# A decode step's output projection: seven rows to a partition in two wo tiles, and their other rows in 8 KB pieces by indirect loads

## The chip, the cores and the metric

The kernel runs on one core of a Trainium2 chip. The metric is the device time of one launch in microseconds. Five engines work side by side: PE (TensorE, matrix products), DVE (VectorE), ACT (ScalarE), POOL (GpSimd) and SP (SyncE, which here only issues transfers). Sixteen DMA engines move data between the chip's memory and the core's on-chip memory of 128 partitions.

## The reference

One decode step of a transformer block with adaptive layer norm, batch 8, width 512, all in float32. The matrix that this change is about is `wo`, of 4096 rows by 512 columns.

```python
W = min(4096, max(256, Sk // 4))          # 2048 of the 8192 cached positions
mod = (silu(c) @ w_mod).reshape(8, 6, 1, 512)
sa, ca, ga, sb, cb, gb = (mod[:, i] for i in range(6))
h = layernorm(x) * (1 + ca) + sa
q = (h @ wq)                              # 32 heads of 128; 8 KV heads
k, v = last W positions of k_cache, v_cache, each KV head for 4 heads
p = softmax(q @ k.T * 128 ** -0.5)
o = (p @ v)                               # (8, 1, 4096)
x = x + ga * (o @ wo)
h = layernorm(x) * (1 + cb) + sb
x = x + gb * (relu(h @ w1 + b1) ** 2 @ w2 + b2)
```

## The kernel before

**Transfers.** Nearly all of the bytes are the caches: K and V of eight KV heads, each in two tiles of 4 MB (`("K", n)` and `("V", n)`, n from 0 to 15). They go into four big slots of one buffer, `home`. A fifth, small slot of 2 MB (`small`) takes in turn the second part of `w_mod`, the wo tiles 0, 1 and 2, the tile `far`, and a part of `w1`. The fourth wo tile comes with the last weights, in a big slot (`tail`). The list `loads` gives the order; `pump` issues the next load of the list as soon as a slot of its size is free, and `done(key)` gives a slot back and pumps. The issues are written into SP's queue in this order, and each waits there for the last reader of its slot.

**Work.** The main loop runs over 37 half-tile steps `s`. In step s, DVE transposes K tile s // 2 (`transposes`, L216), PE makes scores (`scores`, L387) and, five steps later (`PV_LAG`), the weighted sums over V (`weighted`, L473); the soft-max of one KV head is spread over the steps after its scores (`soft_a` to `soft_g`). Every fourth step `gather` turns one head group's result into `oT`, which has, for 128 partitions and 8 chunks i, a column for each batch: partition p, chunk i stands for row 8p + i or, in the first tile, another order (below). Every eighth step `project_o(j)` (L526) multiplies `oT` with wo tile j, of 1024 rows, and adds into `wo_ps`. It runs at steps 14, 22 and 30 for j = 0, 1, 2, and after the loop for j = 3.

**The first wo tile before.** Its 1024 rows are 32 blocks of 32 rows. Of each block, 28 rows go to four partitions, seven rows each (14 KB to a partition, one load); the other four rows of every block, 128 rows in all, make the tile `far`, of 8 KB pieces. The pieces are loaded by three DMAs on SP's queue: two of 12 partitions (L143) and one of 8 (L144), in the partitions 0 to 11, 32 to 43, and 3, 7, ... 31. GpSimd clears half of the slot first (L139). In `project_o(0)`, seven matmuls take the seven chunks, and four matmuls with the selection matrix `fsel` (L537) put the eighth chunk's values into the places of the pieces (`oX`, by two ACT copies). `far_rows` (L549), at step 18, multiplies them with the far tile: eight matmuls, four over 64 partitions and four over 32. `gather` writes the columns in the matching order when `hk < 2`, that is for the first wo tile.

**The second wo tile before** has eight rows to a partition (16 KB), one load (L133), and eight matmuls.

**The end.** After the loop come the last projection, the second layer norm, the MLP with w1 and w2 (L690 takes the 14 chunks of w2, whose last pieces are the last loads of all), and the store of y (L700). The biases b1 and b2 are loaded on ACT's queue by two DMAs, four partitions each (L563).

Of the kernel before, what the change touches and what calls it, by code (L numbers as in the profile page):

```python
# [8 lines left out]
F32 = mybir.dt.float32  # L9
AF = mybir.ActivationFunctionType  # L10
ALU = mybir.AluOpType
# [2 lines left out]
EPS = 1e-5  # L14
BIG_SLOTS = 4
PV_LAG = 5


@with_exitstack
def tile_adaln_cached_attention_mlp(  # L20
# [14 lines left out]
    nc = tc.nc  # L35
    P = 128
    B, HKV, SK, DH = k_cache.shape
    D = wq.shape[0]
    HQ = wq.shape[1] // DH
    REP = HQ // HKV  # L40
# [8 lines left out]
    H = P // 2  # L49
# [3 lines left out]
    consts = ctx.enter_context(tc.tile_pool(name="consts", bufs=1))  # L53
    work = ctx.enter_context(tc.tile_pool(name="work", bufs=2))
    ktp = ctx.enter_context(tc.tile_pool(name="ktp", bufs=2))
    ps_m = ctx.enter_context(tc.tile_pool(name="ps_m", bufs=2, space=bass.MemoryType.PSUM))
# [8 lines left out]
    for q in range(D // P):  # L65
        b = slice(32 * q, 32 * q + B)
        nc.scalar.dma_start(xc_in[b], xc[b])

    ident = consts.tile([P, P], F32, name="ident")
    make_identity(nc, ident)  # L70
    ones = consts.tile([P, P], F32, name="ones")
    nc.gpsimd.memset(ones, 1.0)
    eps = consts.tile([P, 1], F32, name="eps")
    nc.vector.memset(eps, EPS)
    fsel = consts.tile([P, 4, P], F32, name="fsel")
    nc.gpsimd.memset(fsel, 0.0)
    for y in range(2):
        nc.gpsimd.tensor_copy(
            fsel[:, :, 32 * y : 32 * y + 12].rearrange("p r (q a) -> p r q a", a=4),
            ident.rearrange("p (y a r q) -> p y r q a", y=2, a=4, r=4)[:, y, :, :3],  # L80
        )
    nc.gpsimd.tensor_copy(
        fsel[:, :, H : H + 32].rearrange("p r (h x) -> p r h x", x=4)[..., 3],
        ident.rearrange("p (h r q) -> p r h q", r=4, q=4)[..., 3],
    )
    oX = consts.tile([P, 8, 32], F32, name="oX")

# [2 lines left out]
    base = [3 * big, 0, big, 2 * big]  # L92
# [10 lines left out]
    def load(key):  # L103
        kind, i = key
        held[key] = free[size_of(key)].pop(0)
        if key == ("wq", 0):
            return
        t = slots[size_of(key)][held[key]]
        if kind in "KV":

            hk, c = divmod(i, 2)
            v = k_cache[4 * c : 4 * c + 4, hk] if kind == "K" else v_cache[c::2, hk]
            v = v[:, SK - W :, :].rearrange("u (p j) d -> p u (j d)", j=NJ)
            cuts = (0, big // 2, big) if key == ("V", 2 * HKV - 1) else (0, big)
            for x, y in zip(cuts, cuts[1:]):
                nc.sync.dma_start(t[:, x:y], v[..., x:y])
            return

        def rows(o, v):
            n = v.shape[1] * v.shape[2]  # L120
            nc.sync.dma_start(t[:, o : o + n].rearrange("p (a n) -> p a n", n=v.shape[2]), v)

        w1v = w1.rearrange("(p kc) n -> p kc n", p=P)

        def wo_rows(j):

            r = 2 * REP * DH
            if j == 0:
                v = wo[:r].rearrange("(b s) n -> b s n", s=32)[:, :28].rearrange("b (g i) n -> b g (i n)", i=7)
                nc.sync.dma_start(t[:, : 7 * D], v)  # L130
                return
            v = wo[j * r : (j + 1) * r, :].rearrange("(p i) n -> p (i n)", p=P)
            nc.sync.dma_start(t[:, : big // 2], v)  # L133

        if kind == "wo":
            wo_rows(i)
        elif kind == "far":

            nc.gpsimd.memset(t[:H], 0.0)  # L139
            v = wo[: 2 * REP * DH].rearrange("(h q s) n -> q h s n", q=4, s=32)[:, :, 28:]  # L140
            v = v.rearrange("q h r n -> q h (r n)")
            for y in range(2):
                nc.sync.dma_start(t[32 * y : 32 * y + 12, : 4 * D], v[:3, 4 * y : 4 * y + 4])  # L143
            nc.sync.dma_start(t[3:32:4, 4 * D :], v[3])  # L144
        elif kind == "mod":

            v = w_mod.rearrange("(p kc) n -> p (kc n)", p=P)
            nc.sync.dma_start(t, v[:, big:] if i else v[:, :big])
        elif kind == "wq":

            o = base[held["wq", 0]]
            nc.sync.dma_start(home[:, o : o + 2 * big], wq.rearrange("(p k) n -> p (k n)", p=P))
        elif kind == "tail":
            wo_rows(HKV // 2 - 1)
            rows(big // 2, w1v[:, 0:2])
        elif kind == "w1":
            rows(0, w1v[:, 2:4])
        else:
            v = w2.rearrange("(p c) n -> p c n", p=P)
            for lo, hi in ((0, 8), (8, 12), (12, 13), (13, 14)):  # L160
                rows(D * lo, v[:, lo:hi])

    def slot(key, n, o=0):

        t = slots[size_of(key)][held[key]][:, o:]
        return t[:, : t.shape[1] // n * n].rearrange("p (a n) -> p a n", n=n)

    loads = [("mod", 0), ("mod", 1), ("wq", 0), ("wq", 1), ("K", 0), ("K", 1)]
    for n in range(2, 2 * HKV):
        if n == 9:  # L170
            loads.append(("far", 0))
        if n in (4, 11, 13):
            loads.append(("wo", (4, 11, 13).index(n)))
        loads += [("K", n), ("V", n - 2)]
    loads += [("V", 2 * HKV - 2), ("V", 2 * HKV - 1), ("tail", 0), ("w1", 0), ("w2", 0)]
    at = [0]
# [6 lines left out]
    def done(*keys):  # L183
        for k in keys:
            free[size_of(k)].append(held.pop(k))
        pump()
# [81 lines left out]
    for k in (2, 3, 4):  # L268
        n = 1 << k
# [223 lines left out]
    def gather(hk):  # L493

        o = OS_.pop(hk)
        b = slice(H * (hk % 2), H * (hk % 2) + H)
        pp = ps_m.tile([P, 512], F32, name="m_ps", tag="m_ps")
        for x in range(2):
            to = pp[b].rearrange("p (d x e i) -> p x e d i", x=2, e=2, i=8)[:, x]
            cuts = [(to, o.rearrange("p e (d i) -> p e d i", i=8))]  # L500
            if hk < 2:
                o = o.rearrange("p e (q s) -> p (e q) s", s=32)
                cuts = [
                    (to[..., :7], o[:, :, :28].rearrange("p a (g i) -> p a g i", i=7)),
                    (to[..., 7].rearrange("p e (r q) -> p e q r", r=4), o[:, :, 28:]),
                ]
            for dest, src in cuts:
                nc.tensor.matmul(dest, pick[:, x].rearrange("p t u -> p (t u)"), src, start=True, stop=True)  # L508
        tr = work.tile([P, 2, 8, 32], F32, name="tr", tag="b", bufs=1)
        nc.vector.transpose(  # L510
            tr[b].rearrange("p e i (x d) -> p (e i) x d", x=2),
            pp[b].rearrange("p (d x e i) -> p (e i) x d", x=2, e=2, i=8),
        )
        nc.vector.tensor_mul(
            oT[b, :, :B].rearrange("p i (w e) -> p e i w", e=2),
            tr[b, :, :, :4],
            RZ_[hk][b].rearrange("p (w e) -> p e w", e=2)[:, :, None, :].to_broadcast([H, 2, 8, 4]),
        )

    def project_o(j):  # L520

        last = j == HKV // 2 - 1
        key = ("tail", 0) if last else ("wo", j)
        w = slot(key, D)
        for i in range(8 if j else 7):
            nc.tensor.matmul(  # L526
                wo_ps[32 * (i % 4) : 32 * (i % 4) + 32, :],
                oT[:, i, :],
                w[:, i, :],
                start=(j == 0 and i < 4),  # L530
                stop=(last and i >= 4),
            )
        if j == 0:

            px = ps_m.tile([P, 512], F32, name="m_ps", tag="m_ps")
            for r in range(4):
                nc.tensor.matmul(px[:, 32 * r : 32 * r + 32], fsel[:, r], oT[:, 7, :], start=True, stop=True)  # L537
            px = px[:, :P].rearrange("p (r b) -> p r b", b=32)
            nc.scalar.copy(oX[:H, :4], px[:H])
            nc.scalar.copy(oX[:32, 4:], px[H : H + 32])  # L540
        if not last:
            done(key)

    def far_rows():

        w = slot(("far", 0), D)
        for r in range(8):
            k = H if r < 4 else 32
            nc.tensor.matmul(  # L549
                wo_ps[32 * (r % 4) : 32 * (r % 4) + 32, :], oX[:k, r], w[:k, r, :], start=False, stop=False  # L550
            )
        done(("far", 0))

    def late_tiles():

        late = work.tile([P, NJ, 8, 4], F32, name="pr4", bufs=1).rearrange("p j x w -> p (j x w)")
        rT = late[:, : FC * 32].rearrange("p (c b) -> p c b", b=32)
        b1_in, b2_in, x1, h2T = late[:NQ, 512 : 512 + FG], late[:NQ, 1024:1152], late[:, 1152:1280], late[:, 1280:1408]
        h2T = h2T.rearrange("p (c b) -> p c b", b=32)
        nc.gpsimd.memset(rT, 0.0)  # L560
        for t, v in ((b1_in, b1), (b2_in, b2)):
            v = v.rearrange("(g n) -> g n", g=NQ)
            nc.scalar.dma_start(t, v)  # L563
        return rT, b1_in, b2_in, x1, h2T

    window(0)
# [2 lines left out]
    for s in range(N + PV_LAG + 1):  # L569
# [16 lines left out]
            soft_f(g - 1)  # L586
        if v > C and v % (2 * C) == 1 and v < N:
            project_o(v // C // 2 - 1)
        if s == 18:
            far_rows()  # L590
        if 1 <= v <= N:
            weighted(v - 1, 1)
        if i == 0 and soft:
# [143 lines left out]
```

## Time and profile before

| | |
|---|---|
| Median of three runs | 393.38 us (393.16 to 393.44) |
| The profiled execution | 393.28 us, of which the profile's span covers 391.5 us |
| PE, DVE, ACT, POOL busy | 258.8, 224.0, 46.7, 5.9 us |
| Bytes moved | 165.04 MB, 422 GB/s over the span |
| DMA queue q1 (SP's) | 6814 packets, 164.70 MB, 98.3% of sixteen engines' span |
| Mean granted clock of PE | 0.886 |

A busy time of an engine is the sum of its instructions; the page's rows of 40 slices show where it lies. A line such as `L526 PE MATMUL wo_ps<-small,oT 128*32 128x512 f32 x16` reads: the instruction of line 526 on PE, writing `wo_ps` from `small` and `oT`, with its shapes and its count. "PEld" is PE's loading of the stationary operand, a name with q (SPq, ACTq) is the engine's queue issuing a transfer, and what stands in brackets is the idle time before an instruction and what ended it. In a table by stretches the columns are the stretch, its length, busy time and count of PE, PEld, DVE, ACT and POOL, the granted clock, the DMA engines' mean busy share and GB/s.

### The profile page before, as it was taken

How to read it: one execution, taken by the hardware profiler on the slowest of the kernel's cores; microseconds unless marked ns; L12 is line 12 of the kernel's file. 1: busy time of each engine (PE TensorE's matmuls, PEld its weight loads, DVE VectorE, ACT ScalarE, POOL GpSimd, SP SyncE). 2: the span in 40 equal slices, each digit the busy share in tenths (PEclk: the TensorE clock that was granted, in tenths of full speed). 3: DMA queues.
4: the chain of work that ended last, by engine and by line, in shares of the span. 5: the costliest groups of instructions: out<-in, count | busy, mean ns of one | idle time of the engine just before them, and what ended most of it. 6: DMA issues, size and time to landing. Idle time of an engine off the chain costs nothing.

```text
span 391.5 us, 4765 instructions
## 1 busy us (share of the span) xinstructions
PE 258.8 (66%) x2050; PEld 79.7 (20%) x2050; DVE 224.0 (57%) x314; ACT 46.7 (12%) x91; POOL 5.9 (2%) x13
## 2 busy tenths in 40 slices
PE   0080959868437873797379828783773737996896
PEld 0030210112112320232122202220221212222333
DVE  1370099878057835874577456490776357854322
ACT  0120111311003100310031003100200003004010
POOL 1000000000000000030000000000000000000000
PEclk9996889998859996999599968988796969997999
DMA  8999999999999999999999999999999999999994
GB/s 330 437 429 426 437 435 442 435 424 411 431 432 432 437 432 435 430 427 429 444 417 435 430 432 432 427 429 427 415 445 437 429 429 431 425 423 424 421 432 190
DMA packets 6915, 165.04 MB, mean 422 GB/s; under 512 B 806, under 2 KB 974, under 8 KB 1230
## 3 DMA queue, kind: packets, MB, share of 16 engines
q1 hardware_dynamic: 6814, 164.70, 98.3%
q8 instruction: 16, 0.26, 0.3%
q10 hardware_dynamic: 80, 0.04, 0.0%
q14 instruction: 5, 0.04, 0.0%
HBM read 164.67 MB, written 0.07 MB: 421 GB/s over the span
## 4 chain that ended last, share of the span: by engine, by line
DMA 59%; DVE 22%; PE 14%; issue 4%; SPq 0%; ACT 0%; DVEq 0%; ACTq 0%
DMA home<-in_A_k_cache_dram 37%; DVE kT L216 12%; DMA home<-in_A_wq_dram 9%; DMA home<-in_B_w_dram 7%; DMA home<-in_A_v_cache_dram 6%; PE s_ps L387 5%; DVE pT L453 4%; PE p_ps L418 3%; PE m_ps L332 2%; PE o_ps L473 2%; DVE pr L446 2%; DVE mx L401 1%; DVE qbd L350 1%; PE m_ps L403 1%; PE m_ps L423 1%
## 5 line engine op out<-in xcount | busy, mean ns | idle before, releaser
L216 DVE STREAM_TRANSPOSE kT<-home 128x1024 f32<-128x1024 f32 x128 | 151.3, 1220 | 81.8 <-DMA home<-in_A_k_cache_dram 77.7
L387 PE MATMUL s_ps<-kT,qst 128*32 128x512 f32 x512 | 129.1, 1075 | 18.9 <-DVE kT L216 18.5
L473 PE MATMUL o_ps<-home,pT 128*32 128x256 f32 x1024 | 70.2, 397 | 11.1 <-DVE pT L453 10.5
L473 PEld LDWEIGHTS o_ps<-home,pT 128*32 128x32 f32 x1024 | 33.8, 118 | 103.1 <-issue 61.3
L403 PE MATMUL m_ps<-ident,mx 128*1 128x128 f32 x16 | 4.3, 364 | 58.3 <-DVE mx L401 58.3
L387 PEld LDWEIGHTS s_ps<-kT,qst 128*32 128x32 f32 x512 | 14.4, 115 | 38.2 <-DVE kT L216 30.1
L453 DVE STREAM_TRANSPOSE pT<-pr 128x2048 f32<-128x2048 f32 x8 | 18.2, 2275 | 1.0 <-ACT pr L436 1.0
L436 ACT ACTIVATE pr<-pr,own 128x512 f32<-128x512 f32 x16 | 17.8, 1223 | 0.3
L430 ACT ACTIVATE pr<-p_ps,nm 128x512 f32<-128x512 f32 x8 | 5.5, 687 | 96.2 <-DVE nm L427 96.2
L397 ACT COPY ss<-s_ps 128x512 f32<-128x512 f32 x8 | 4.7, 586 | 98.1 <-issue 69.2
L332 PE MATMUL m_ps<-home,oX 128*32 128x512 f32 x64 | 9.2, 741 | 10.1 <-DMA home<-in_A_wq_dram 10.1
L375 ACT COPY qst<-q_ps 32x128 f32<-32x128 f32 x32 | 8.2, 256 | 62.9 <-PE q_ps L364 62.6
L350 DVE COPY qbd<-m_ps 32x128 f32<-32x128 f32 x8 | 3.0, 373 | 18.8 <-PE m_ps L347 18.6
L403 PEld LDWEIGHTS m_ps<-ident,mx 128*1 128x1 f32 x16 | 0.7, 81 | 63.5 <-DVE mx L401 63.5
L250 PE MATMUL m_ps<-xsum,sel 128*128 128x1 f32 x2 | 0.6, 362 | 18.5 <-DVE xsum L248 18.5
L418 PE MATMUL p_ps<-ss,perm 128*128 128x512 f32 x16 | 11.8, 829 | 0.0
L427 DVE TENSOR_SCALAR nm<-m_ps 128x1 f32<-128x1 f32 x8 | 1.3, 158 | 16.4 <-PE m_ps L423 16.4
L508 PE MATMUL m_ps<-o_sb,pick 128*64 128x256 f32 (+2 forms) x40 | 9.7, 377 | 0.9 <-DVE o_sb L491 0.9
L446 DVE TENSOR_SCALAR pr<-pr,own 128x512 f32<-128x512 f32 x16 | 9.2, 657 | 0.8 <-ACT pr L430 0.8
L510 DVE STREAM_TRANSPOSE tr<-m_ps 64x512 f32<-64x512 f32 x8 | 5.7, 714 | 5.4 <-PE m_ps L508 5.2
L490 DVE TENSOR_SCALAR o_sb<-o_ps,bit 128x128 f32<-128x128 f32 x16 | 5.2, 327 | 5.5 <-PE o_ps L473 5.4
L228 DVE TENSOR_SCALAR e_sb<-e_sb 128x128 f32<-128x128 f32 x1 | 0.2, 227 | 12.9 <-ACT e_sb L227 12.9
(134 smaller groups left out, 131.7 us busy)
## 6 DMA issues: line engine op xcount, KB each, us to landing
home<-in_A_k_cache_dram SPq DMA_DIRECT2D x16, 4096.0 KB, 36.6
home<-in_A_v_cache_dram SPq DMA_DIRECT2D x15, 4096.0 KB, 22.4
home<-in_w_mod_dram SPq DMA_DIRECT2D x1, 4096.0 KB
small<-in_A_wo_dram SPq DMA_DIRECT2D x2, 2048.0 KB, 25.4
home<-in_A_v_cache_dram SPq DMA_DIRECT2D x2, 2048.0 KB, 21.5
small<-in_w_mod_dram SPq DMA_DIRECT2D x1, 2048.0 KB
home<-in_A_wo_dram SPq DMA_DIRECT2D x1, 2048.0 KB
home<-in_B_w_dram SPq DMA_DIRECT2D x1, 2048.0 KB
```

What stands on the lines that cost most here:

```text
L216: nc.vector.transpose(KTS[q, j][:, rows], k[:, rows, 32 * j : 32 * j + 32])
L332: nc.tensor.matmul(pqs[r][32 * g : 32 * g + 32, :], hT[:, kc, :], w[:, 4 * r + g, :], start=(kc == 0), stop=(kc == NQ - 1),)
L350: nc.vector.tensor_copy(qbd[b, 4 * r : 4 * r + 4, j].rearrange("p g (b t) -> p t g b", t=REP), pT_[b].rearrange("p (t g b) -> p t g b", t= ...
L375: nc.scalar.copy(own[b, :, :, i, 0], pq[b, :P].rearrange("p (c m t) -> p c m t", c=2, t=REP))
L387: nc.tensor.matmul(s_ps[0][32 * g : 32 * g + 32, :], qst[hk % 2][:, P * (4 * c + u) + 32 * j :][:, :32], kT[:, u], start=(c == 0 and j == ...
L403: nc.tensor.matmul(MX_[hk][0:1, :P], mx, ident, start=True, stop=True)
L418: nc.tensor.matmul(sp, perm, SS_.pop(hk), start=True, stop=True)
L436: nc.scalar.mul(X_[hk][..., w], pr, own[:, w : w + 1])
L446: nc.vector.tensor_scalar(X_[hk][..., w], pr, own[:, w : w + 1], None, op0=ALU.mult)
L453: nc.vector.transpose(PT_[hk].rearrange("p e j r -> p j e r"), X_.pop(hk).rearrange("p j x w -> p j (x w)"))
L473: nc.tensor.matmul(O_[n][32 * g : 32 * g + 32, : 2 * DH], PT_[hk][:, e, j : j + 2].rearrange("p j r -> p (j r)"), vt[:, j : j + 2, :].rear ...
L508: nc.tensor.matmul(dest, pick[:, x].rearrange("p t u -> p (t u)"), src, start=True, stop=True)
```

## The change

- The second wo tile is laid out as the first: seven rows to a partition in one load, and its other 128 rows in a far tile of its own, `("far", 1)`, which passes through the small slot between wo tiles 1 and 2. `project_o(1)` has seven matmuls and the four selections, `far_rows(1)` runs at step 25. wo tile 2 is listed one K tile later.
- Both far tiles are loaded by an indirect DMA from GpSimd's queue. Each partition has a row index (`pieces`) into wo seen as 1024 rows of 8 KB; 32 partitions have a piece, the other 96 an index beyond wo's end, which is left out. The partitions come from `GROUPS`: 64 to 67, 92 to 95, 28 to 31, 16 to 19, 0 to 11, and 96, 124, 60 and 40. By the change's description this makes ten or eight pieces, over both tiles, on each of seven DMA engines.
- The indices are made on the chip: GpSimd writes them as a row with eleven iotas, a matmul with a single 1 turns it into a column, and two DVE steps store it as integers for tile 0 and tile 1.
- `fsel` follows GROUPS, with eleven copies instead of three. GpSimd clears all 128 partitions of the far tile's 8 KB instead of 64 partitions of 16 KB. `far_rows` is four matmuls over 128 partitions, and one ACT copy serves instead of two.
- b1 is loaded in three DMAs (partitions 0 and 1, 2, 3) and b2 in two.

```diff
+GROUPS = ((64, 4), (92, 4), (28, 4), (16, 4), (0, 4), (4, 4), (8, 4), (96, 1), (124, 1), (60, 1), (40, 1))
...
+    pieces = consts.tile([P, 2], mybir.dt.int32, name="pieces")
+
+    row = consts.tile([1, P], F32, name="row")
+    nc.gpsimd.memset(row, 4.0 * D)
+    ways, n = [], 0
+    for m, k in GROUPS:
+        h, q = divmod(n, 4)
+        ways.append((slice(m, m + k), h, slice(q, q + k)))
+        nc.gpsimd.iota(
+            row[:, m : m + k],
+            pattern=[[8, k]],
+            base=32 * h + 8 * q + 7,
+            channel_multiplier=0,
+            allow_small_or_imprecise_dtypes=True,
+        )
+        n += k
+    assert n == 32
+    pr_ = ps_m.tile([P, 512], F32, name="m_ps", tag="m_ps")
+    nc.tensor.matmul(pr_[:, 0:1], row, ones[0:1, 0:1], start=True, stop=True)
+    nc.vector.tensor_copy(pieces[:, 0:1], pr_[:, 0:1])
+    nc.vector.tensor_scalar(pieces[:, 1:2], pr_[:, 0:1], 2.0 * P, None, op0=ALU.add)
     nc.gpsimd.memset(fsel, 0.0)
...
+    for to, h, q in ways:
+        nc.gpsimd.tensor_copy(fsel[:, :, to], ident.rearrange("p (h r q) -> p r h q", h=8, r=4)[:, :, h, q])
...
-            if j == 0:
-                v = wo[:r].rearrange("(b s) n -> b s n", s=32)[:, :28].rearrange("b (g i) n -> b g (i n)", i=7)
+            if j < 2:
+                v = wo[j * r : (j + 1) * r].rearrange("(b s) n -> b s n", s=32)[:, :28].rearrange("b (g i) n -> b g (i n)", i=7)
                 nc.sync.dma_start(t[:, : 7 * D], v)
...
-            nc.gpsimd.memset(t[:H], 0.0)
-            v = wo[: 2 * REP * DH].rearrange("(h q s) n -> q h s n", q=4, s=32)[:, :, 28:]
-            v = v.rearrange("q h r n -> q h (r n)")
-            for y in range(2):
-                nc.sync.dma_start(t[32 * y : 32 * y + 12, : 4 * D], v[:3, 4 * y : 4 * y + 4])
-            nc.sync.dma_start(t[3:32:4, 4 * D :], v[3])
+            nc.gpsimd.memset(t[:, : 4 * D], 0.0)
+            nc.gpsimd.indirect_dma_start(
+                out=t[:, : 4 * D],
+                out_offset=None,
+                in_=wo.rearrange("(a r) n -> a (r n)", r=4),
+                in_offset=bass.IndirectOffsetOnAxis(ap=pieces[:, i : i + 1], axis=0),
+                bounds_check=wo.shape[0] // 4 - 1,
+                oob_is_err=False,
+            )
...
-        if n == 9:
-            loads.append(("far", 0))
-        if n in (4, 11, 13):
-            loads.append(("wo", (4, 11, 13).index(n)))
+        if n in (9, 13):
+            loads.append(("far", n // 13))
+        if n in (4, 11, 14):
+            loads.append(("wo", (4, 11, 14).index(n)))
         loads += [("K", n), ("V", n - 2)]
...
-            if hk < 2:
+            if hk < 4:
...
-        for i in range(8 if j else 7):
+        for i in range(8 if j > 1 else 7):
...
-        if j == 0:
+        if j < 2:
...
-            nc.scalar.copy(oX[:H, :4], px[:H])
-            nc.scalar.copy(oX[:32, 4:], px[H : H + 32])
+            nc.scalar.copy(oX[:, :4], px)
...
+    def far_rows(j):
+
+        w = slot(("far", j), D)
+        for r in range(4):
             nc.tensor.matmul(
-                wo_ps[32 * (r % 4) : 32 * (r % 4) + 32, :], oX[:k, r], w[:k, r, :], start=False, stop=False
+                wo_ps[32 * r : 32 * r + 32, :], oX[:, r], w[:, r, :], start=False, stop=False
             )
-        done(("far", 0))
+        done(("far", j))
...
-        for t, v in ((b1_in, b1), (b2_in, b2)):
+        for t, v, cuts in ((b1_in, b1, (0, 2, 3, 4)), (b2_in, b2, (0, 2, 4))):
             v = v.rearrange("(g n) -> g n", g=NQ)
-            nc.scalar.dma_start(t, v)
+            for x, y in zip(cuts, cuts[1:]):
+                nc.scalar.dma_start(t[x:y], v[x:y])
...
-        if s == 18:
-            far_rows()
+        if s in (18, 25):
+            far_rows(s // 25)
```

More of the change, by code (lines that the diff above doesn't have):

```diff
@@ L75, in tile_adaln_cached_attention_mlp @@
     fsel = consts.tile([P, 4, P], F32, name="fsel")
-    nc.gpsimd.memset(fsel, 0.0)
-    for y in range(2):
[L78 to L86, printed above, removed]
+    oX = consts.tile([P, 8, 32], F32, name="oX")
+    pieces = consts.tile([P, 2], mybir.dt.int32, name="pieces")
[18 more added lines that the diff above has]
+    nc.vector.tensor_scalar(pieces[:, 1:2], pr_[:, 0:1], 2.0 * P, None, op0=ALU.add)
+    nc.gpsimd.memset(fsel, 0.0)
+    for to, h, q in ways:
+        nc.gpsimd.tensor_copy(fsel[:, :, to], ident.rearrange("p (h r q) -> p r h q", h=8, r=4)[:, :, h, q])
     big = NJ * DH
@@ L137, in load @@
         elif kind == "far":
-            nc.gpsimd.memset(t[:H], 0.0)
-            v = wo[: 2 * REP * DH].rearrange("(h q s) n -> q h s n", q=4, s=32)[:, :, 28:]
-            v = v.rearrange("q h r n -> q h (r n)")
-            for y in range(2):
-                nc.sync.dma_start(t[32 * y : 32 * y + 12, : 4 * D], v[:3, 4 * y : 4 * y + 4])
-            nc.sync.dma_start(t[3:32:4, 4 * D :], v[3])
+            nc.gpsimd.memset(t[:, : 4 * D], 0.0)
[7 more added lines that the diff above has]
+            )
         elif kind == "mod":
@@ L538, in project_o @@
             px = px[:, :P].rearrange("p (r b) -> p r b", b=32)
-            nc.scalar.copy(oX[:H, :4], px[:H])
-            nc.scalar.copy(oX[:32, 4:], px[H : H + 32])
+            nc.scalar.copy(oX[:, :4], px)
         if not last:
             done(key)
[L544 to L548, printed above, removed]
+    def far_rows(j):
+        w = slot(("far", j), D)
+        for r in range(4):
             nc.tensor.matmul(
-                wo_ps[32 * (r % 4) : 32 * (r % 4) + 32, :], oX[:k, r], w[:k, r, :], start=False, stop=False
+                wo_ps[32 * r : 32 * r + 32, :], oX[:, r], w[:, r, :], start=False, stop=False
             )
-        done(("far", 0))
+        done(("far", j))
     def late_tiles():
```

## The prediction

> **What bounds the kernel now.** I read the page's engine row, its row of slices and its queue rows first, then the table by stretches.
>
> ```profile
> PE 258.8 (66%) x2050; PEld 79.7 (20%) x2050; DVE 224.0 (57%) x314; ACT 46.7 (12%) x91; POOL 5.9 (2%) x13
> DMA  8999999999999999999999999999999999999994
> q1 hardware_dynamic: 6814, 164.70, 98.3%
> q8 instruction: 16, 0.26, 0.3%
> DMA 59%; DVE 22%; PE 14%; issue 4%; SPq 0%; ACT 0%; DVEq 0%; ACTq 0%
> 40.00:380.00 340.00, 240.14 (x1842) 71.26 (x1834) 209.80 (x258) 42.24 (x82) 3.98 (x2) 0.88 1.00 430
> ```
>
> No compute engine is busy for more than two thirds, DMA holds 59% of the chain that ended last, and the DMA row is full from the second slice to the last but one. The last row is a stretch of 340 us: its DMA share is 1.00, at 430 GB/s. The transfers never run dry, so the kernel is 164.70 MB behind one full queue. A K tile of 4,096 KB is 9.8 us of that. An edit that leaves the bytes alone can gain only where the sixteen DMA engines do not finish together. One engine moves 430/16 = 26.9 GB/s: 8 KB is 0.305 us of one engine, 16 KB 0.61 us, 64 KB 2.44 us, 80 KB 3.05 us.
>
> Do they finish together? The same table in stretches of 1 us at the end (DMA share is the last column but one):
>
> ```profile
> 383.00:384.00 1.00, 1.00 (x4) 0.36 (x2) 0.68 (x3) 0.00 (x0) 0.00 (x0) 1.00 0.89 358
> 384.00:385.00 1.00, 1.00 (x25) 0.64 (x28) 0.00 (x0) 0.00 (x0) 0.00 (x0) 1.00 0.82 340
> 385.00:386.00 1.00, 1.00 (x45) 1.00 (x40) 0.00 (x0) 0.00 (x0) 0.00 (x0) 1.00 0.72 274
> 386.00:387.00 1.00, 0.64 (x24) 0.37 (x20) 0.00 (x0) 0.00 (x0) 0.00 (x0) 1.00 0.71 272
> 387.00:388.00 1.00, 1.00 (x40) 0.74 (x33) 0.00 (x0) 0.00 (x0) 0.00 (x0) 1.00 0.10 35
> ```
>
> They don't. Idle are 0.11 x 16 = 1.8 engines from 383 on, 2.9 from 384 and 4.5 from 385 to 387; the other eleven or twelve work to about 387.2 to 387.4. The shares add up to 3.24 us, so sixteen engines that ended together would end near 386.25: some 1.1 us is the most that a better spread can bring. Four or five engines have 2 to 3.5 us in hand.
>
> The end follows the last piece of w2 directly:
>
> ```profile
> 383.55 0.28 DVE L683 SCALAR_TENSOR_TENSOR pr<-relu 128x112 f32<-128x112 f32 x1
> 384.36 1.95 PE L690 MATMUL m_ps<-home,pr 128*32 128x128 f32 x64
> 386.67 1.72 PE L690 MATMUL m_ps<-home,pr 128*32 128x128 f32 x48 [0.36 <-DMA home<-in_B_w_dram]
> 387.96 0.16 PEld L690 LDWEIGHTS m_ps<-home,pr 128*32 128x32 f32 x8 [0.26 <-DMA home<-in_B_w_dram]
> ```
>
> L690 waits for w2 at 386.67 and again at 387.96, and only y and its store come after. Would compute take over if w2 came sooner? VectorE's last step is done at 383.83, so PE could go through 64 matmuls in 1.95 us and 48 in 1.72 - 0.26 us, and be done at 387.2 instead of 388.4. A gain of up to 1.1 us at the DMA therefore arrives at the end whole.
>
> **The change, part by part.** *Bytes.* Before, an engine carried 112 KB of wo's first tile (seven rows of 2 KB on 128 partitions, over sixteen engines) and 128 KB of the second (eight rows); the first tile's other 256 KB, the far rows, lay where three small loads put them. Now both tiles are 112 KB per engine, and 512 KB of far rows come in 64 pieces of 8 KB, by the change's description on seven engines: ten (80 KB) on four of them, eight (64 KB) on three. The sum is the same. Each of the nine engines without pieces loses 16 KB: 0.61 us earlier, and 0.305 us more for each far piece that it had. Each of the seven gains 80 - 16 = 64 KB or 48 KB, 2.44 or 1.83 us, less what it carried of the far rows before. No view of the profile names the engine of a packet, so which of the seven are among the four or five early ones is open; the price on either side is what I have. If the four with a real gain are the early ones, their 1.8 to 2.4 us fit into 2 to 3.5 us in hand, and the last engine is one of the nine: the end moves by -0.61 us. The bounds are -1.1 us (all together) and +2.44 us (a late engine that had no far rows gets ten pieces).
>
> The Trainium skill's page "DMA: Bandwidth & Descriptors" (Why a DMA increments its semaphore by 16 and not by 1) lets a load from SP use the largest count up to 16 that divides the slowest dimension of both sides. By it the two loads of 12 partitions ran on three engines and that of eight on eight, 72 KB on each of three engines; its section The descriptor swizzle, applied to the new partitions, puts the pieces on engines 0, 1, 2, 4, 7, 8 and 15, the first three being those. Three of the seven would then get -24 to -8 KB and only four 40 to 64 KB, an estimate of 1.5 to 2.4 us; the sum stays -0.6 us. The section speaks of plain loads to 128 partitions, and no run here shows it for an indirect one.
>
> *The packets' other queue.* The pieces come on GpSimd's queue between packets of q1. The nearest rows lie far apart. Queue q8's 16 packets of 16 KB take 0.3% of sixteen engines' span, 0.003 x 16 x 391.5/16 = 1.2 us each against 0.61 us by the byte. Queue q10's packets, from memory into a tile as the pieces are, stand in this answer for 5 to 14 us:
>
> ```profile
> q1 hardware_dynamic: 158, 3.85, 99.8%
> q10 hardware_dynamic: 64, 0.03, 1.2%
> ```
>
> Together 101.0% at an unbroken rate, 0.012 x 16 x 9/64 = 27 ns a packet. So a piece costs between nothing and, scaled from q8's excess of 0.6 us on 16 KB, 0.3 us beyond its bytes. I take nothing, since the destination and kind are q10's; ten pieces at 0.3 us would be 3 us on the seven.
>
> *The far loads and who waits.*
>
> ```profile
> 168.80 1.92 PE L526 MATMUL wo_ps<-small,oT 128*32 128x512 f32 x14
> 170.79 3.51 POOL L139 MEMSET small<- 64x4096 f32 x1 [168.18 <-PE wo_ps L526]
> 179.24 1.69 SPq L143 DMA_DIRECT2D small<-in_A_wo_dram  x2
> 180.97 0.69 SPq L144 DMA_DIRECT2D small<-in_A_wo_dram  x1
> 208.77 2.05 PE L549 MATMUL wo_ps<-small,oX 64*32 64x512 f32 x16
> 249.17 1.92 PE L526 MATMUL wo_ps<-small,oT 128*32 128x512 f32 x16
> 262.26 0.58 SPq L133 DMA_DIRECT2D small<-in_A_wo_dram  x1
> 283.72 0.54 SPq L116 DMA_DIRECT2D home<-in_A_v_cache_dram  x1
> 335.64 1.92 PE L526 MATMUL wo_ps<-small,oT 128*32 128x512 f32 x16
> small<-in_A_wo_dram SPq DMA_DIRECT2D x2, 2048.0 KB, 25.4
> 247.20 25.85 DMA home<-in_A_k_cache_dram
> 289.98 26.80 DMA home<-in_A_k_cache_dram
> ```
>
> SP loses three issues (2.4 us of a queue that is ahead of the transfers). GpSimd's memset is 128 x 2,048 instead of 64 x 4,096, half of 3.51 us, and its load follows at about 173 instead of 179 to 182; far_rows reads at 208.8, 35 us later. The second far tile is loaded after L526's reads at 249.2 to 251.1, at about 254. It is wanted at step 25, just ahead of the weighted sums that release the V issue of 283.72: some 28 us of cover. Through q1 a wo tile took 25.4 us; on its own queue it needn't stand behind K and V. Should it be late, PE waits, the weighted sums queued behind it too, and V's slot with them. wo's third tile then waits in the one small slot until that far_rows: its issue moves from 262.3 to about 284.3, behind that V. Nothing stands behind it on SP that could go, since the next K goes out at 290. Between 262 and 284 the queue holds 2 MB (4.9 us) less; a K issued at 247.2 needs 25.85 us, 9.8 of them its own, so 16 us of work stand ahead of it and 11 us would be left: the queue stays full. The tile is read at 335.6, 51 us after the new issue. Cost of it all: nothing; without that cover, the lateness itself.
>
> *Compute.* project_o(1) sheds one matmul and gains the four of fsel, far_rows is twice four instead of eight. The PE rows above give 1.92/16 = 0.12 us an instruction; each matmul is two: 6 more instructions, under 1 us of a PE that is 34% idle. ACT has as many copies. b1 and b2 go in five loads instead of two on ACT's queue:
>
> ```profile
> 358.14 0.60 ACTq L563 DMA_DIRECT2D pr<-in_B_b_dram  x2
> L660 PE MATMUL m_ps<-pr,bsel x2: 534/586/638, 376.4 to 376.9; 4*128 4x448 f32 x2
> ```
>
> Three issues more are 0.9 us on ACT's queue, 18 us ahead of b1's reader, with packets like q10's: nothing; without that cover L660 waits, and the MLP with it.
>
> *Start.* GpSimd gets a memset, eleven small iotas and eleven copies for three; a matmul and two VectorE steps wait for the iotas, ahead of VectorE's sel.
>
> ```profile
> L78 POOL COPY fsel<-ident 128x48 f32<-128x48 f32 x2 | 0.5, 257 | 0.1
> 13.87 1.28 ACT L227 ACT_TABLE_LOAD   x1 [13.87 <-DMA xc_in<-in_xc_dram]
> 18.54 0.59 PE L250 MATMUL m_ps<-xsum,sel 128*128 128x1 f32 x2 [18.54 <-DVE xsum L248]
> ```
>
> Twelve steps of 0.26 us are 3 us; VectorE can't go on to the first matmul's operand until ACT's result, after 15 us, and PE's first matmul of before is at 18.5. Iotas of 0.7 us would still fit. Free.
>
> **Sum.** 0 for compute, start and waits, -0.61 us for the nine engines: 393.28 - 0.61 = 392.67 us of the profiled execution, whose time is 0.10 us under the median; I say 392.7.
>
> **Rivals.** *A late engine gets the pieces* (slower). Place: one of the seven is among the eleven that end at 387. Price: ten pieces less the row, +2.44 us, 395.7 to 395.8; eight pieces 395.1. It decides as soon as an engine that carried no far rows has less than 1.8 us in hand. For it: five early engines by the rows against up to seven wanted. Against: the old far rows lie on some of the seven, which pays part. 0.12.
>
> *The pieces cost more than bytes* (slower). At q8's excess the seven get 3 us more: 392.7 + 3 = 395.7, where those in hand are used up; from 0.13 us a piece on the result is slower than before by 0.2%, from 0.06 us it is level. For it: q8. Against: q10. 0.13. The same skill page (Latency and other measured facts) calls engines 7 and 15 usually slower, with GpSimd's descriptor rings as its guess, and both would be in the seven; no run here shows it.
>
> *The pieces don't go to seven engines.* Spread over all sixteen each engine gets 32 - 16 = 16 KB more unless it had far rows: +0.61 us, 393.9. Nothing in the trace shows how an indirect load is dealt out over the engines; the partitions chosen, in groups of four, speak for a rule that the kernel relies on. 0.10.
>
> *Better than the nine.* If those that end last had a far piece too, they are 0.92 us earlier: 392.4, at best 392.2. 0.25, which leaves 0.40 for the forecast itself.
>
> **How the numbers follow.** 0.2% is 0.8 us, about what a measurement of this kernel can tell from no change. Faster by more means under 392.6: the better case and a part of the forecast, 0.25 + 0.08 = 0.33. Within: the rest of the forecast and the even spread, 0.32 + 0.07 = 0.39. Slower: the two rivals and a part of the spread, 0.28. The range goes from the bound 392.2 up to 395.2, which takes in the even spread, a late engine with eight pieces and extra costs up to 0.25 us a piece, and leaves out the dearer half of the two slow rivals; the likeliest case alone spans 392.4 to 393.1.
>
> **What would show it.** Right: the shares from 383 to 387 nearer to 1.00 and then a steeper fall, L690's last wait ending near 387.3, the full stretch at 430 GB/s still. Wrong: a lone tail of 0.1 to 0.4 in share after 388 (late engines), the GpSimd queue's row with over 0.35 us for an 8 KB packet (dear pieces), PE waiting at far_rows, or a K wait on VectorE that grows after 284.

## The result

The changed kernel takes 392.80 us (392.62 to 393.06, 22 runs) beside 393.37 us (393.16 to 393.49, 22 runs) of the kernel before on the same chip: a ratio of 0.9986 [0.998, 0.9992], 0.57 us less. The forecast was 392.7 with a gain of 0.61 us. The profiled execution took 392.73 us, its span 390.9 us (before: 393.28 and 391.5).

The page of the changed kernel: the engine row, the slices of the DMA engines, the queues (packets, MB, share of sixteen engines' span) and the chain that ended last.

```profile
PE 260.2 (67%) x2066; PEld 81.8 (21%) x2066; DVE 224.2 (57%) x316; ACT 46.7 (12%) x91; POOL 10.2 (3%) x36
DMA  8999999999999999999999999999999999999995
q1 hardware_dynamic: 6768, 164.17, 98.1%
q0 software_dynamic: 288, 0.53, 0.4%
DMA 53%; DVE 23%; PE 18%; issue 5%; ACT 1%; SPq 0%; ACTq 0%; DVEq 0%
```

The 0.53 MB that left SP's queue q1 now stand in GpSimd's queue q0, and sixteen instructions more on PE and 4.3 us more on POOL did not lengthen anything. The transfers are still what the kernel waits for. Now the stretches of its end, with the columns of before (DMA share last but one):

```profile
40.00:380.00 340.00, 242.52 (x1874) 73.49 (x1866) 210.10 (x259) 42.58 (x83) 6.24 (x5) 0.89 1.00 430
383.00:384.00 1.00, 0.42 (x16) 0.45 (x20) 0.00 (x0) 0.00 (x0) 0.00 (x0) 1.00 1.02 426
384.00:385.00 1.00, 1.00 (x46) 1.00 (x41) 0.00 (x0) 0.00 (x0) 0.00 (x0) 1.00 1.06 420
385.00:386.00 1.00, 0.56 (x24) 0.29 (x16) 0.00 (x0) 0.00 (x0) 0.00 (x0) 1.00 0.88 340
386.00:387.00 1.00, 1.00 (x40) 1.00 (x40) 0.00 (x0) 0.00 (x0) 0.00 (x0) 1.00 0.53 199
387.00:388.00 1.00, 0.69 (x20) 0.16 (x8) 0.23 (x1) 0.00 (x0) 0.00 (x0) 1.00 0.00 0
```

The rate from 40 to 380 us is what it was. The end is another: before, the share fell in steps, 0.89, 0.82, 0.72, 0.71, 0.10; now it is full to 385 and is gone at 387. The view counts a packet whole where it starts, so a share can pass 1.00. What the earlier end does to the last matmuls, in the timeline:

```profile
381.85 0.28 DVE L700 SCALAR_TENSOR_TENSOR pr<-relu 128x112 f32<-128x112 f32 x1
383.58 1.96 PE L707 MATMUL m_ps<-home,pr 128*32 128x128 f32 x64 [0.85 <-DMA home<-in_B_w_dram]
385.97 1.73 PE L707 MATMUL m_ps<-home,pr 128*32 128x128 f32 x48 [0.44 <-DMA home<-in_B_w_dram]
387.27 0.16 PEld L707 LDWEIGHTS m_ps<-home,pr 128*32 128x32 f32 x8 [0.27 <-DMA home<-in_B_w_dram]
388.41 0.35 SPq L717 DMA_DIRECT2D out_dram<-y  x1
```

L707 is the loop that was L690, L717 the store that was L700, and L700 is now VectorE's step that was L683. The last wait for w2 ends at 387.27 instead of 387.96, 0.69 us earlier, and the store is issued 0.70 us earlier by its row. The span is 0.6 us shorter: the last 0.1 us is given back after the store's issue.

### The profile page after: what moved, and what is told of

It reads as the page before. It is cut to its first block, busy times and chain, and to the rows that moved or that the text cites. A ratio compares the mean times of both kernels' runs of the same rounds, so it can differ in the third digit from the quotient of the medians.

```text
span 390.9 us, 4829 instructions
## 1 busy us (share of the span) xinstructions
PE 260.2 (67%) x2066; PEld 81.8 (21%) x2066; DVE 224.2 (57%) x316; ACT 46.7 (12%) x91; POOL 10.2 (3%) x36
## 4 chain that ended last, share of the span: by engine, by line
DMA 53%; DVE 23%; PE 18%; issue 5%; ACT 1%; SPq 0%; ACTq 0%; DVEq 0%
DMA home<-in_A_k_cache_dram 37%; DVE kT L234 12%; DMA home<-in_A_wq_dram 9%; PE s_ps L405 6%; DMA home<-in_B_w_dram 5%; DVE pT L471 5%; PE p_ps L436 3%; PE o_ps L491 3%; PE m_ps L350 2%; DVE pr L464 2%; DMA pr<-in_B_b_dram 2%; DVE mx L419 1%; PE m_ps L421 1%; DVE qbd L368 1%; PE m_ps L441 1%
## 5 line engine op out<-in xcount | busy, mean ns | idle before, releaser
L491 PE MATMUL o_ps<-home,pT 128*32 128x256 f32 x1024 | 68.5, 390 | 10.8 <-DVE pT L471 10.5
L436 PE MATMUL p_ps<-ss,perm 128*128 128x512 f32 x16 | 12.9, 896 | 0.0
L526 PE MATMUL m_ps<-o_sb,pick 128*64 128x224 f32 (+2 forms) x48 | 9.9, 345 | 0.9 <-DVE o_sb L509 0.9
L154 POOL MEMSET small<- 128x2048 f32 x2 | 3.6, 1802 | 240.8 <-PE wo_ps L544 240.8
```

The source lines that it names most:

```text
L436: nc.tensor.matmul(sp, perm, SS_.pop(hk), start=True, stop=True)
L491: nc.tensor.matmul(O_[n][32 * g : 32 * g + 32, : 2 * DH], PT_[hk][:, e, j : j + 2].rearrange("p j r -> p (j r)"), vt[:, j : j + 2, :].rear ...
```

## Experiments

The prediction's own theory: the end is set by the last of the sixteen DMA engines, nothing but the bytes on each engine counts, and the gain is the 16 KB that nine engines lost. Its rivals: the gain comes from the queue (SP's queue is relieved, the far tile no longer stands behind K and V); from the layout of the compute and of the loads; or from all bytes together, in which case it does not matter who carries them. Each comparison below has the kernel before on the same chip at 393.31 to 393.39 us; "over the changed kernel" means over 392.80 us.

**The pieces spread over all sixteen engines** (two in each group of four partitions):

```diff
-GROUPS = ((64, 4), (92, 4), (28, 4), (16, 4), (0, 4), (4, 4), (8, 4), (96, 1), (124, 1), (60, 1), (40, 1))
+GROUPS = tuple((4 * (e % 8) + 64 * (e // 8), 2) for e in range(16))
```

> The pieces lie evenly: two of each tile on every one of the sixteen engines (groups of two partitions), all else as in the changed kernel. Theory A, spread: the end is set by the engine that ends last, and the gain came from taking 16 KB off nine engines. Those nine now get four pieces, 32 KB at 26.9 GB/s, 1.22 us more: 392.8 + 1.2 = 394.0, slower than before. Theory B, queue: the gain came from the far loads leaving SP's queue and from the second tile's layout, wherever the pieces lie: 392.8.

**The pieces on eight other engines**, which by the theory are among the late ones, eight pieces each:

```diff
+GROUPS = tuple((m, 4) for m in (20, 24, 68, 72, 76, 80, 84, 88))
```

> All pieces on eight of the nine engines that had none (partitions 20 to 27 and 68 to 91, by the same grouping of partitions), eight pieces each over both tiles. Theory A: those engines get 64 KB more than in the changed kernel, 2.44 us: 395.2, and the end shows a tail of about half the engines. Theory B: 392.8. If the placement does not follow the partitions, nothing changes either: 392.8.

**A staircase**: 14, 12, 10, 8, 8, 6, 4 and 2 pieces on eight engines:

```diff
+GROUPS = ((12, 4), (20, 4), (68, 4), (72, 4), (76, 4), (80, 3), (88, 1), (44, 3), (104, 1), (84, 2), (100, 2))
```

> Another number of pieces on each engine, to see whether the placement by partitions can be steered one by one: per tile seven pieces in the groups of partitions 12 to 15 and 44 to 46, six in 68 and 100, five in 72 and 104, four in 76 and 20, three in 80, two in 84, one in 88. Theory A: the engine with fourteen pieces in all gets 112 KB, 4.27 us, and sets the end at 397.1, or, if it is the one that had up to 2 us in hand, the one with twelve does at 396.5; the fall of the DMA share at the end is a staircase. Theory B: 392.8 and a steep fall.

Measured: even 394.23 us (394.05 to 394.56), ratio 1.0022 [1.0013, 1.0032]; late 395.22 us (395.08 to 395.24), 1.0045 [1.0032, 1.0059]; graded 396.38 us (396.31 to 396.45, two runs), 1.0076 [1.0058, 1.0095]. Work, queue and bytes are those of the changed kernel; only the partitions differ, and with their groups the number of iotas and copies at the start (sixteen each in even, eight in late, eleven as before in graded). The table by stretches, first late, then graded:

```profile
387.00:388.00 1.00, 1.00 (x48) 1.00 (x40) 0.00 (x0) 0.00 (x0) 0.00 (x0) 1.00 0.47 176
388.00:389.00 1.00, 0.91 (x35) 0.64 (x28) 0.00 (x0) 0.00 (x0) 0.00 (x0) 1.00 0.46 174
389.00:390.00 1.00, 0.99 (x39) 0.72 (x32) 0.00 (x0) 0.00 (x0) 0.00 (x0) 1.00 0.04 14
```

```profile
387.00:388.00 1.00, 1.00 (x22) 0.52 (x24) 0.00 (x0) 0.00 (x0) 0.00 (x0) 1.00 0.43 170
388.00:389.00 1.00, 1.00 (x47) 1.00 (x40) 0.00 (x0) 0.00 (x0) 0.00 (x0) 1.00 0.34 115
389.00:390.00 1.00, 0.80 (x30) 0.53 (x26) 0.00 (x0) 0.00 (x0) 0.00 (x0) 1.00 0.13 49
390.00:391.00 1.00, 0.99 (x40) 0.73 (x34) 0.00 (x0) 0.00 (x0) 0.00 (x0) 1.00 0.03 12
```

In late, 0.47 x 16 = 7.5 engines work on until 389 and then stop together: eight engines carry the load. In graded the share comes down step by step. The prices follow the bytes of the fullest late engine: even puts 32 KB more on each of the nine than the change does, 1.22 us by 0.61 us for 16 KB, measured 1.43; late 64 KB, 2.44 us, measured 2.42; graded 3.58 us, which is 12 pieces (96 KB, 3.66 us) and not 14 (4.27 us); that fits if the fullest engine is one with time in hand, which is argued and not shown. So where 512 KB go is worth up to 3.6 us here, with everything else equal. The Trainium skill's page "DMA: Bandwidth & Descriptors" (The descriptor swizzle) gives the engine from the partition in groups of four, for a plain load of 128 partitions; the partitions of these three kernels were chosen by it. For the indirect load these runs agree with it: 7.5 engines in late's row, eight by the section.

**The change in the first wo tile only**; the second as before, eight rows to a partition and no far tile:

```diff
-            if j < 2:
+            if j == 0:
...
-        if n in (9, 13):
-            loads.append(("far", n // 13))
-        if n in (4, 11, 14):
-            loads.append(("wo", (4, 11, 14).index(n)))
+        if n == 9:
+            loads.append(("far", 0))
+        if n in (4, 11, 13):
+            loads.append(("wo", (4, 11, 13).index(n)))
...
-            if hk < 4:
+            if hk < 2:
...
-        for i in range(8 if j > 1 else 7):
+        for i in range(8 if j else 7):
...
-        if s in (18, 25):
-            far_rows(s // 25)
+        if s == 18:
+            far_rows(0)
```

> The first tile as in the changed kernel, the second tile as before: eight rows to a partition, no second far tile. Theory A: the nine engines without pieces get 16 KB back, 0.61 us: 393.4, level with before, although the indirect load is there. Theory B, queue: the far loads have left SP's queue here too, 392.8. Theory C, layout: each tile of seven rows brings half of the gain, 393.1.

Measured: 393.27 us (393.16 to 393.54), ratio 1.0 [0.9991, 1.0009]. The new queue, the indirect load, the split biases and an SP queue without the three small loads are all there, and the median gains 0.05 us, which is nothing beside the interval. All eleven runs lie above theory C's 393.1, though the interval of the ratio takes it in. Its end:

```profile
386.00:387.00 1.00, 0.79 (x32) 0.53 (x24) 0.00 (x0) 0.00 (x0) 0.00 (x0) 1.00 0.61 219
387.00:388.00 1.00, 1.00 (x39) 0.74 (x32) 0.00 (x0) 0.00 (x0) 0.00 (x0) 1.00 0.11 39
```

The tail of 0.11 after 387 is the one of before (0.10). It goes only when the second tile's eighth row leaves the late engines; the queue alone is not the reason.

**No piece is moved**: the iotas are left out, so every index lies beyond wo. The far rows' part of the product is not computed.

```diff
-        nc.gpsimd.iota(
-            row[:, m : m + k],
...
-        )
```

> All 128 indices point beyond wo, so that the indirect loads bring none of the 512 KB of far rows (that part of the projection is left out); all else as in the changed kernel. Theory A, spread: the nine engines without pieces set the end and they are left as they were, 392.7 to 392.8, and the DMA share at the end falls to about 9 of 16 engines. Theory D, bytes: the kernel is its bytes through one full queue, 512 KB less are 1.2 us: 391.6.

Measured: 392.78 us (392.57 to 392.99), ratio 0.9986 [0.9977, 0.9995]: 512 KB less, and the time is that of the changed kernel. Its q0 row and its end:

```profile
q0 software_dynamic: 288, 0.00, 0.0%
384.00:385.00 1.00, 1.00 (x47) 1.00 (x40) 0.00 (x0) 0.00 (x0) 0.00 (x0) 1.00 0.61 252
385.00:386.00 1.00, 0.65 (x24) 0.38 (x16) 0.00 (x0) 0.00 (x0) 0.00 (x0) 1.00 0.51 191
386.00:387.00 1.00, 0.93 (x36) 0.93 (x40) 0.00 (x0) 0.00 (x0) 0.00 (x0) 1.00 0.32 121
387.00:388.00 1.00, 0.80 (x24) 0.26 (x12) 0.13 (x1) 0.00 (x0) 0.00 (x0) 1.00 0.00 0
```

From 384 on only some ten engines work, then eight, then five; the rest are idle, and the end is where it was. The bytes of the seven are free, which is what the change rests on, and total bytes set nothing here.

**b1 and b2 in one load each**, the rest as changed:

```diff
-        for t, v, cuts in ((b1_in, b1, (0, 2, 3, 4)), (b2_in, b2, (0, 2, 4))):
+        for t, v, cuts in ((b1_in, b1, (0, 4)), (b2_in, b2, (0, 4))):
```

> b1 and b2 in one load each over four partitions, as before, instead of five loads; all else as in the changed kernel. Theory A: two packets of some 75 and 27 ns move from engine to engine, nothing beyond 0.1 us, 392.8. Rival: the split of the biases is part of the gain, then up to 393.1.

**The split alone**, in the kernel before:

```diff
-        for t, v in ((b1_in, b1), (b2_in, b2)):
+        for t, v, cuts in ((b1_in, b1, (0, 2, 3, 4)), (b2_in, b2, (0, 2, 4))):
...
-            nc.scalar.dma_start(t, v)
+            for x, y in zip(cuts, cuts[1:]):
+                nc.scalar.dma_start(t[x:y], v[x:y])
```

> The kernel before, with only the five loads of b1 and b2 instead of two. If the split helps by itself, as the 0.2 us that the changed kernel lost without it suggest: 393.1. If it helps only where an engine with ten pieces is the last, as theory A says: 393.3, since in the kernel before the last engines are others.

Measured: b_whole 393.04 us (392.96 to 393.22), ratio 0.9993 [0.9984, 1.0002]: 0.24 us over the changed kernel, whose interval overlaps with this one, and 0.26 us over no_pieces, which keeps the split and ran beside it on the same chip. The split alone 393.70 us (393.49 to 393.87), ratio 1.0009 [1.0001, 1.0018], 0.3 us slower than before. The stores, b_whole first, then the split alone:

```profile
388.57 0.35 SPq L717 DMA_DIRECT2D out_dram<-y  x1
```

```profile
389.02 0.35 SPq L701 DMA_DIRECT2D out_dram<-y  x1
```

With the split the store is 0.16 us earlier in the changed kernel (388.41) and 0.09 us earlier in the one before (389.11): a small help in both up to there. So both expectations for the split alone, 393.1 and 393.3, were missed. Its store even lands earlier: by the trace's record of single packets its last one ends at 390.23 us, in the kernel before at 390.31. Against that, this profile of the split alone ends 391.7 - 389.02 = 2.7 us after that issue, the kernel before 391.5 - 389.11 = 2.4. Why the end after the store is longer stays open, and with it whether the split is worth 0.2 us on its own.

**The pieces as plain loads on ACT's queue**, eleven for each tile, to the same partitions:

```diff
-            nc.gpsimd.indirect_dma_start(
...
-            )
+            v, b = wo.rearrange("(a s) n -> a s n", s=32)[:, 28:].rearrange("a r n -> a (r n)"), 32 * i
+            for m, k in GROUPS:
+                nc.scalar.dma_start(t[m : m + k, : 4 * D], v[b : b + k])
+                b += k
```

> The same pieces in the same partitions, but loaded by eleven plain loads for each tile on ACT's queue instead of one indirect load on GpSimd's. If partitions decide the engine whatever the queue: 392.8. If a plain load takes as many engines as its partitions allow (the rule of the Trainium skill's page DMA: Bandwidth & Descriptors, Why a DMA increments its semaphore by 16 and not by 1: lowest-numbered four for four partitions, one for one), the 64 pieces lie on four engines, 22 on the first and 14 on three others. Against eight on the first now that is 14 more, 14 x 0.305 = 4.3 us: 397.1.

Measured: 402.11 us (401.43 to 403.38), ratio 1.0228 [1.0212, 1.0244], 5 us over the expectation. ACT's timeline and three stretches:

```profile
175.22 16.63 ACTq L157 DMA_DIRECT2D small<-in_A_wo_dram  x9
191.97 0.59 ACT L411 COPY ss<-s_ps 128x512 f32<-128x512 f32 x1 [16.71 <-DMA small<-in_A_wo_dram]
```

```profile
40.00:380.00 340.00, 235.13 (x1808) 71.14 (x1800) 206.49 (x247) 41.45 (x79) 4.08 (x3) 0.87 1.00 422
260.00:270.00 10.00, 6.48 (x67) 2.03 (x62) 6.04 (x7) 0.00 (x0) 0.00 (x0) 1.00 0.97 330
394.00:395.00 1.00, 1.00 (x44) 0.89 (x35) 0.00 (x0) 0.00 (x0) 0.00 (x0) 1.00 0.21 74
```

Three things went wrong at once. An issue takes 0.26 us, but the last nine of the first tile's eleven stretch over 16.6 us, and ACT's next work comes at 191.97, where it comes at 183.48 in the changed kernel. The rate over the 340 us fell from 430 to 422, which by itself is 340 x 8/422 = 6.4 us; while the second tile's pieces come, from 260 to 270, it is 330 GB/s, at a share of 0.97. And the tail is 0.21 x 16 = 3 to 4 engines wide: the pieces do not lie on seven engines, and four were expected. Which of the three cost how much isn't told apart.

**Even spread by one plain load on SP's queue** (32 partitions), to leave GpSimd's queue out:

```diff
+GROUPS = tuple((m, 4) for m in range(0, 32, 4))
...
+            v = wo.rearrange("(a s) n -> a s n", s=32)[:, 28:].rearrange("a r n -> a (r n)")
+            nc.sync.dma_start(t[:32, : 4 * D], v[32 * i : 32 * i + 32])
...
+        if n in (9, 12):
+            loads.append(("far", n // 12))
```

> Both far tiles in the partitions 0 to 31, each by one plain load of 32 partitions on SP's queue instead of the indirect load (the second is listed one K tile earlier). Theory A, with 32 partitions spread over all sixteen engines: as in the kernel with evenly placed pieces, 394.2, whichever queue carries them. Rival, queue: GpSimd's own queue is part of the gain, then over 394.6. Rival: SP's wait for the second far tile's slot lets the queue run dry, then the DMA share or the rate from 40 to 380 us falls below 1.00 and 430 GB/s, and the time is over 395.

Measured: 397.74 us (397.43 to 398.3), ratio 1.0114 [1.0099, 1.0128]. SP's timeline, then the same K tile's issue in the changed kernel:

```profile
252.47 0.32 SPq L156 DMA_DIRECT2D small<-in_A_wo_dram  x1
252.88 0.54 SPq L131 DMA_DIRECT2D home<-in_A_k_cache_dram  x1
```

```profile
245.47 0.54 SPq L131 DMA_DIRECT2D home<-in_A_k_cache_dram  x1
```

SP waits for the small slot until 252.5, and the K tile behind it goes out at 252.88 instead of 245.47. That looks like the price of a far tile on SP's queue, but the stretches say otherwise; the last row is that of the even kernel, where its second far tile comes:

```profile
195.00:200.00 5.00, 4.84 (x44) 1.42 (x42) 3.00 (x6) 2.68 (x4) 0.00 (x0) 1.00 1.06 342
250.00:280.00 30.00, 14.92 (x136) 5.13 (x127) 12.52 (x13) 1.88 (x6) 1.80 (x1) 0.83 1.01 407
260.00:265.00 5.00, 5.00 (x44) 1.18 (x36) 4.65 (x6) 0.00 (x0) 0.00 (x0) 1.00 1.03 308
```

```profile
255.00:260.00 5.00, 3.88 (x28) 1.25 (x32) 5.00 (x5) 0.00 (x0) 0.00 (x0) 0.74 1.01 433
```

After the late issue, from 250 to 280, the share stays at 1.01: the queue does not run dry. The rate falls where the pieces flow, to 342 GB/s for the first far tile, whose issue held nobody up (the K tile behind it went out at 181.91, in the changed kernel at 181.30), and to 308 for the second, with the share over 1.00 both times. So no engine is idle there, but packets take longer: by the record of single packets 1.59 and 1.71 us for 32 KB of K or V against 1.22 elsewhere, and 0.45 and 0.48 us for a piece. These ten microseconds alone cost 5 x 88/430 + 5 x 122/430 = 2.4 us of the 3.5 by which this kernel is slower than the even one. Why plain loads into the partitions 0 to 31 slow the others isn't shown. SP's queue alone doesn't do it: the kernel before loads its pieces there too, at 0.31 us each, and has 431 GB/s from 195 to 205, where they flow. Whether GpSimd's queue is worth anything by itself is left open by this run.

**More instructions on PE.** The late engines of before could be late because of q8, whose 16 packets of 16 KB each bring PE's instructions. 128 small matmuls whose result nobody uses, four instructions each (two on PE, two on PEld), were added in two ways: four in each of 32 steps (the diff) and eight in each of the first 16.

```diff
+        if s < N:
+            more = ps_1.tile([P, 512], F32, name="q_ps")
+            for _ in range(4):
+                nc.tensor.matmul(more[:, 0:1], row, ones[0:1, 0:1], start=True, stop=True)
```

> 128 small matmuls more (four in each of 32 steps, 512 instructions, result unused); all else as in the changed kernel. Theory A with q8 as the cause of the late engines: 512 instructions are two more q8 packets of 16 KB before the end, on engines that end last; each costs its engine at least the 1.2 us of the page's row, 394.0 to 394.3, with q8 at 18 packets, while the DMA share from 40 to 380 us stays 1.00. Rival: q8's packets do not set which engine is late, 392.8. Rival: PE, busier by 30 us or more, holds the slots: the share falls below 1.00 and the time rises by more than 2 us.

> The 128 small matmuls again (512 instructions, result unused), but eight in each of the first 16 steps, so that PE is as free at the end as in the changed kernel. Theory A with q8 as the cause of late engines: 18 packets in q8, one of the two that come on top falls on an engine that ends last, whose last transfer lands 1.2 to 1.5 us later than now: 394.0 to 394.3, with one engine alone busy in the last microsecond (a share of 0.06). Rival, PE time: the extra matmuls cost nothing once they lie early, 392.8.

Measured: 395.04 us (394.64 to 396.0), ratio 1.005 [1.0036, 1.0064], and 394.26 us (393.81 to 397.51, 12 runs), 1.0032 [1.0017, 1.0048]. The first one's timeline and a stretch, then rows of the second:

```profile
386.74 3.26 PE L711 MATMUL m_ps<-home,pr 128*32 128x128 f32 x112
387.00:388.00 1.00, 1.00 (x48) 1.00 (x41) 0.00 (x0) 0.00 (x0) 0.00 (x0) 1.00 0.06 25
```

```profile
q8 instruction: 18, 0.29, 0.3%
40.00:380.00 340.00, 270.76 (x2104) 103.80 (x2100) 210.69 (x258) 42.30 (x82) 6.24 (x5) 0.91 1.00 429
387.76 1.69 PE L711 MATMUL m_ps<-home,pr 128*32 128x128 f32 x48 [0.47 <-DMA home<-in_B_w_dram]
```

In the first, PE runs all 112 matmuls without a wait for w2: PE itself set the end, and the time doesn't answer. Its share does in part: 0.06 is one engine of sixteen, and by the single packets that engine ends w2 at 388.3, 1.3 us after the last of the others. In the second the wait for w2 is back, q8 has two packets more, and the end is 1.46 us over the changed kernel, where the row of before gave 1.2 us a packet. But the rate over the 340 us is 429 instead of 430, and one in 430 is 0.8 us. By the single packets w2 ends 1.8 us later in the profiled execution than in that of the changed kernel (388.55 and 386.78), but most of the engines too end some 0.8 us later, so only the rest can be the work of one late engine. That q8's packets make engines late is supported by this, not shown.

## Why the prediction was right

*What bounds it.* Held: rate 430 in both kernels, no_pieces at the same median with 512 KB less, even to graded with the time by the bytes of one engine.

*Nine engines lose 16 KB, 0.61 us.* Held in kind, less surely in size: 0.57 us in the median and 0.69 us at the last wait, but both figures include the split of the biases. Of two kernels with the split, half, which lacks the loss, gains 0.05 us and the changed one 0.57, 0.52 us apart. Of two without it, the kernel before and b_whole, the latter is only 0.27 us faster (393.31 and 393.04), with an interval that takes in no change. That the sum came within 0.04 us is partly luck.

*What the seven get fits into the 2 to 3.5 us in hand.* Held, and this was the open step: the share stays full to 385 and then falls at once. No row of the kernel before tells which engines are early, so it held by the change's choice of partitions and not by a reading; the forecast had given it 0.40. The same number of bytes on engines without anything in hand is the late kernel at 395.22, within the 395.1 to 395.8 that the rival gave.

*The pieces' price.* Taken as their bytes alone, 0.305 us each. The changed kernel's DMA answer for 176 to 183 us, where the first far tile flows:

```profile
q1 hardware_dynamic: 97, 2.65, 88.3%
q0 software_dynamic: 88, 0.26, 9.4%
```

0.094 x 16 x 7 = 10.5 us for 32 pieces and 56 packets of four bytes (left-out rows for the most part): at most 0.33 us a piece. Packet by packet the trace has 0.313 us on average. The dear rival (0.6 us a piece) fell.

*Far loads, waits and start.* Held as far as they can be seen; GpSimd's timeline:

```profile
1.66 0.93 POOL L86 IOTA row<- 1x4 f32 x11
170.27 1.80 POOL L154 MEMSET small<- 128x2048 f32 x1 [165.59 <-PE wo_ps L544]
172.36 1.17 POOL L155 DMA_INDIRECT small<-in_A_wo_dram,pieces  x1 [0.29 <-POOL small L154]
250.80 1.00 POOL L155 DMA_INDIRECT small<-in_A_wo_dram,pieces  x1 [0.28 <-POOL small L154]
```

The loads go out at 172.4 and 250.8, where the prediction had 173 and 254; the eleven iotas take 0.93 us.

*Compute that doesn't take over.* Held, but its room was read too wide. The prediction let PE begin at 383.83, where VectorE's step ends. Its row has PE at 384.36, and 384.36 + 1.95 + 1.46 = 387.8, so that only 0.6 us of a gain could have arrived, not 1.1. In the changed kernel VectorE's step comes at 381.85 instead of 383.55, and PE's row of L707 waits for w2 and no longer for VectorE; why the step comes 1.7 us earlier isn't followed here.

*The split biases.* Taken as nothing; by b_whole they help the changed kernel by 0.24 us, two fifths of the whole gain, and the kernel before gains nothing by them. That term was mis-sized, and its cause is not settled; the 16 KB alone may then be worth less than their 0.61 us.

*Better than the nine* (392.4) did not come, and little of it is left. By the single packets fifteen engines end w2 between 386.26 and 386.78, one at 384.70. The shares from 384 on, 1.06 + 0.88 + 0.53 = 2.47 us, would have sixteen engines end together near 386.5: an even end could bring some 0.3 us more.

## What to carry to other kernels

When a queue is always full, read the last few microseconds in stretches of one: a share that falls in steps says that the DMA engines do not end together, and the area under one minus the share is what a better spread can bring. Then bytes matter only on the engines that end last: 512 KB taken off the early ones brought nothing, 16 KB off each of the late ones, with the split of the biases, 0.57 us, and another choice of partitions cost 1.4 to 3.6 us. Read the GB/s beside the share: with the pieces as plain loads the rate fell to 308 GB/s at a share of 1.03, and the share alone doesn't show that.

## What was not expected of the hardware

Left-out rows of an indirect load are counted as read. The changed kernel's page, then that of the kernel before:

```profile
HBM read 166.24 MB, written 0.07 MB: 425 GB/s over the span
```

```profile
HBM read 164.67 MB, written 0.07 MB: 421 GB/s over the span
```

The 1.57 MB more are 192 rows of 8 KB, and 2 x 96 indices lie beyond wo. In no_pieces, where all rows are left out, all 288 packets of q0 take under 0.05% of sixteen engines' 390 us, so at most 11 ns each.

Loads of up to four partitions on ACT's queue, issued while the DMA engines were full, put off ACT's next work by 8.5 us at the first far tile (191.97 instead of 183.48), though an issue itself takes 0.26 us; the indirect load held GpSimd for 1.2 us.
